# Earlier and mostly unpaced routing scatters, a first slot prepared by quarters, weights' loads ahead of its numbers

## The chip, the cores and the metric

The kernel runs on one core of a Trainium2 chip. The metric is device time in microseconds (us) from launch to end; lower is better. The engines are TensorE (PE), VectorE (DVE), ScalarE (ACT), GpSimd (POOL) and SyncE (SP); SP mostly issues DMAs. Each engine runs its own stream in the order in which the program was written, and waits on semaphores for the others.

## The reference

Three layers follow one another, all in float32.

1. Linear attention over q, k, v of shape (8, 8, 576, 64): `softmax(q)` along the head dimension, `softmax(k)` along the sequence, `kv = k_s^T v` per head, and `q_s kv`. The result is read as x with 4608 tokens of 512 numbers.
2. A mixture of 8 experts with one expert per token: `logits = x @ w_gate + bias[modality]`, the expert is the argmax, its softmax weight scales the token, and `out = gate * relu(x @ w1[e]) @ w2[e]`, w1 being 512x1024 and w2 1024x512.
3. A dense layer pair, 512 to 2048 to 512, with a leaky relu of slope 0.01; its weights arrive as float64.

## The kernel before, in words

**Attention and routing (lines 96 to 417).** Batches are taken in four pairs, each of nine chunks of 128 tokens, so 36 chunks. A chunk is transposed and exponentiated (`trans`, line 232), multiplied with its pair's `kv` (`xmm`, 239; `xp` has two buffers), divided by its sums and written to DRAM as `xd` (`evac`, 255). The last chunk of a pair takes its two halves from two batches (lines 247 to 251). Beside that, `phase_k` (137) prepares the next pair's `kv`, and `phase_q` (209) subtracts row maxima from q, in three thirds of a pair: `qmax` on DVE (218), `qsub` on POOL (222).

Routing (`phase_r`, 275) takes chunks in five groups: 0 to 8, 9 to 17, 18 to 26, 27 to 32, 33 to 35, numbered 0 to 4 here. Steps r0 to r16 compute for each token its expert, its gate and its row in a table `region` in DRAM that is ordered by expert. Nearly all of them are small DVE operations; `rm` (330) is a tiny matmul and `rx` (311) an ACT exponential. Then one indirect DMA of POOL for each chunk, the scatter (`scat`, 360), writes 128 pairs of token number and gate into `region`. A paced scatter (`paced`, 372) has a one-element POOL copy in front of it that reads the `ri` of a given chunk, so that POOL waits until attention has come that far.

The order is written by hand: every step has a time in units of chunks, the list is sorted by it (line 416), and each engine gets its instructions in that order. `route` (392) adds a group's steps at times relative to its last chunk's end, from a table, and its scatters from `ts` on, `rate` apart.

**Expert tables (`slot_tables`, 425).** From the expert counts DVE computes, in a chain of small operations that ends with the casts into `ti` (475, 476), for each slot of 512 tokens its expert, its place in `region`, and its place in the output.

**Experts (`experts`, 485).** Sixteen slots, nine of them always run. For a slot s:
- `idload` (544): SP reads 4 KB of `region` at an address that it takes from `ti`, into `idt`.
- `xload` (549): DVE casts the token numbers, and POOL issues four gathers of 128 rows of `xd` into the quarters of `xg`.
- `xgate` (557): ACT scales each quarter by the gate.
- `xprep(k)` (561): PE transposes block k of all four quarters, and `split` (480) writes it as a high part `xh` (ACT) and a rest `xl` (DVE).
- `wload` (513) loads weights in pieces of 512 KB through a ring of six buffers, on SP, at an address from `ti`. `wsplit` (534) splits a piece into high part and rest (ACT, then DVE) and lets `loads_to` (529) issue more loads. A load into a used buffer waits for the DVE half of that split.
- `pass1` (567) and `pass2` (578) multiply, each product as three matmuls of parts. `pass1` of f needs all 512 columns of `xh` and `xl`, and the w1 piece f // 2.

Between the slots' steps the float64 weights of layer 3 are converted (`conversions`, 640; loads by `f64_load`, 592). Before the first slot the program writes lines 682 to 692: the numbers of slot 0, two weight loads, the numbers of slot 1, three more loads, the gathers, the first w1 split, the gates, the four `xprep`, the other w1 splits.

**Layer 3 (`Hidden` and `last_product`).** The two dense products run after the experts, PE-bound; the change doesn't touch them.

Of the kernel before, what the change touches and what calls it, by code (L numbers as in the profile page):

```python
# [9 lines left out]
F32 = mybir.dt.float32  # L10
# [4 lines left out]
ALU = mybir.AluOpType  # L15
# [4 lines left out]
B, H, S, D = 8, 8, 576, 64  # L20
NT, DM = B * S, H * D
NE, F1, F2 = 8, 1024, 2048
NPAIR = B // 2
# [68 lines left out]
def bc(ap, axis, n):  # L92
    a = ap.unsqueeze(axis)
    shape = list(a.shape)
    shape[axis] = n
    return a.broadcast_to(shape)


def attention(ctx, tc, cst, a, region, xd):

    nc = tc.nc
    ident, onesf, trib, onesb, biasT, tokid = cst["id"], cst["one"], cst["trib"], cst["oneb"], cst["biasT"], cst["tok"]
# [9 lines left out]
    kvx = []  # L112
    for i in range(4):
        t = one.tile([128, 4, 146], F32, name=f"kvx{i}")
# [97 lines left out]
    def phase_q(i):  # L212
        s = {}

        def heads(n):
            return qt[i].rearrange("p c (h d) -> p (c h) d", d=D)[:, 24 * n:24 * n + 24]

        def qmax(n):
            qm = s[n] = sp.tile([128, 24], F32, tag="qm", name="qm")
            nc.vector.tensor_reduce(out=qm, in_=heads(n), axis=AX.X, op=ALU.max)  # L220

        def qsub(n):
            v = heads(n)
            nc.gpsimd.tensor_tensor(out=v, in0=v, in1=bc(s[n][:, :], 2, D), op=ALU.subtract)

        tm, ts = ((0.2, 3.2, 9.5), (1.2, 4.2, 10.5)) if i == 0 else ((4.6, 7.5, 11.0), (5.2, 8.5, 12.0))
        return [(t, qmax, n) for n, t in enumerate(tm)] + [(t, qsub, n) for n, t in enumerate(ts)]

    def phase_x(i):
        s = {}  # L230

        def trans(c):
            tp = ps_t.tile([128, 4, 128], F32, tag="t", name="tq")
            for hp in range(4):
                nc.tensor.transpose(out=tp[:, hp], in_=qt[i][:, c, 128 * hp:128 * hp + 128], identity=ident)
            eq = s["eq", c] = sp.tile([128, 4, 128], F32, tag="eq", name="eq", bufs=3)
            nc.scalar.activation(out=eq, in_=tp, func=AF.Exp)

        def xmm(c):
            eq = s["eq", c]  # L240
            xp = s["xp", c] = ps_x.tile([128, 4, 256], F32, tag="x", name="xp")
            if c < 8:
                kx = kvx[(2 * i + c // 4) % 4]
                for hp in range(4):
                    nc.tensor.matmul(xp[:, hp, 0:146], lhsT=eq[:, hp], rhs=kx[:, hp], start=True, stop=True)
            else:
                for j in range(2):
                    kx = kvx[(2 * i + j) % 4]
                    for hp in range(4):
                        nc.tensor.matmul(xp[64 * j:64 * j + 64, hp, 0:146], lhsT=eq[:, hp, 64 * j:64 * j + 64],  # L250
                                         rhs=kx[:, hp], start=True, stop=True)
            nc.scalar.activation(out=ri[:, NC * i + c], in_=xp[:, :, 144:146], func=AF.Identity, bias=eps[:, 0:1])
            nc.scalar.copy(out=lr[:, NC * i + c], in_=xp[:, :, 128:144])

        def evac(c):
            r = ri[:, NC * i + c]
            nc.vector.reciprocal(out=r, in_=r)
            xr = sp.tile([128, DM], F32, tag="xr", name="xr", bufs=4)
            nc.vector.tensor_tensor(out=xr.rearrange("p (q j d) -> p q j d", q=4, j=2),
                                    in0=s["xp", c][:, :, 0:128].rearrange("p q (j d) -> p q j d", j=2),  # L260
                                    in1=bc(r, 3, D), op=ALU.mult)
            if c < 8:
                r0 = (2 * i + c // 4) * S + 128 * (c % 4)
                nc.sync.dma_start(out=xd[r0:r0 + 128], in_=xr)
            else:
                for j in range(2):
                    r0 = (2 * i + j) * S + 512
                    nc.sync.dma_start(out=xd[r0:r0 + 64], in_=xr[64 * j:64 * j + 64])

        l = []  # L270
        for c in range(NC):
            l += [(c - 0.9, trans, c), (c + 0.3, xmm, c), (c + 1.0, evac, c)]
        return l
# [104 lines left out]
    def add(t0, l):  # L378
        for x in l:
            steps.append((t0 + x[0], len(steps)) + tuple(x[1:]))  # L380
# [11 lines left out]
    def route(c0, c1, times, ts, rate=0.0):  # L392


        fs, scats = phase_r(c0, c1)
        t = 0
        for n, (name, f) in enumerate(fs.items()):
            t = times.get(name, t)
            add(c1 + t, [(0.001 * n, f)])
        for n, (f, c) in enumerate(scats):  # L400
            if rate:
                at = c1 + ts + rate * n
                add(at, [(0.0, paced, min(int(at) - 1, NPAIR * NC - 1), f, c)])
            else:
                add(c1 + ts, [(0.001 * n, f, c)])

    slow = dict(r0=1.15, r1=2.5, r2=3.5, rx=4.4, r5=4.5, r8=5.6, rm=6.55, r10=6.6, r12=7.6, r13=7.61, r16=8.5)
    mid = dict(r0=0.2, r1=0.9, r2=1.2, rx=2.1, r5=2.15, r8=2.6, rm=3.3, r10=3.4, r12=4.1, r16=4.6)
    fast = dict(r0=0.2, r2=0.6, rx=1.45, r5=1.15, rm=2.25, r10=2.1, r12=2.6)
    route(0, 9, slow, 9.05, 1.0)  # L410
    route(9, 18, slow, 9.05, 0.7)
    route(18, 27, mid, 5.05, 0.5)
    route(27, 33, fast, 3.5)
    route(33, 36, dict(r0=0.2), 0.5)
    add(1.0, [(0.1, cst["prep"])])
    for x in sorted(steps, key=lambda x: x[:2]):
# [63 lines left out]
def split(nc, hi, lo, src):  # L480
    nc.scalar.copy(out=hi, in_=src)  # L481
    nc.vector.tensor_tensor(out=lo, in0=src, in1=hi.bitcast(F32), op=ALU.subtract)  # L482


def experts(ctx, tc, cst, a, region, xd, dense, did, wops, pre):
    nc = tc.nc
    ident = cst["id"]
    wp = ctx.enter_context(tc.tile_pool(name="wp", bufs=1, reuse_waits="tile"))
    ps = ctx.enter_context(tc.tile_pool(name="ps_m", bufs=3, space=PSUM, reuse_waits="tile"))
    ps2 = ctx.enter_context(tc.tile_pool(name="ps_m2", bufs=2, space=PSUM, reuse_waits="tile"))  # L490
# [6 lines left out]
    xh = wp.tile([128, 4, SLOT], F32R, name="xh")  # L497
    xl = wp.tile([128, 4, SLOT], F32R, name="xl")
# [4 lines left out]
    idts = [wp.tile([128, 4, 2], F32, name=f"idt{i}") for i in range(3)]  # L503
    idis = [wp.tile([128, 4], I32, name=f"idi{i}") for i in range(2)]
    xg = wp.tile([128, 4, DM], F32, name="xg")
# [4 lines left out]
    def reg(s, f, mx):  # L510
        return nc.values_load(ti[0:1, 3 * s + f:3 * s + f + 1], engines=[SP] + [ACT] * (f == 2), min_val=0, max_val=mx)

    def wload(s, which, c):
        t = stage[s, which, c] = ring[cnt[0] % NST]
        cnt[0] += 1
        if s not in regs:
            regs[s] = reg(s, 0, NE - 1)
        e = bass.ds(regs[s], 1)
        if which == 1:
            src = a["w1"][e, :, 256 * c:256 * c + 256].rearrange("a (k p) f -> p (a k) f", p=128)  # L520
        else:
            src = a["w2"][e, 256 * c:256 * c + 256, :].rearrange("a (k p) f -> p (a k) f", p=128)
        nc.sync.dma_start(out=t.rearrange("p (k f) -> p k f", k=4 if which == 1 else 2), in_=src)
# [5 lines left out]
    def loads_to(n):  # L529
        while nload[0] < min(n, len(items)):  # L530
            wload(*items[nload[0]])
            nload[0] += 1

    def wsplit(s, which, c):
        n = 8 * s + 4 * (which - 1) + c
        loads_to(n + 1)
        t = stage.pop((s, which, c))
        if which == 1:
            split(nc, w1h[:, :, 256 * c:256 * c + 256], w1l[:, :, 256 * c:256 * c + 256], t.rearrange("p (k f) -> p k f", k=4))
        else:  # L540
            split(nc, w2h[:, 2 * c:2 * c + 2], w2l[:, 2 * c:2 * c + 2], t.rearrange("p (k f) -> p k f", k=2))
        loads_to(n + 1 + AHEAD)

    def idload(s):
        if s < NSLOT:
            nc.sync.dma_start(out=idts[s % 3].rearrange("p t c -> p (t c)"),
                              in_=region[bass.ds(reg(s, 1, NE * NT), SLOT), :].rearrange("(p t) c -> p (t c)", t=4))
# [9 lines left out]
    def xgate(s):  # L557
        for t in range(4):
            nc.scalar.activation(out=xg[:, t], in_=xg[:, t], func=AF.Copy, scale=idts[s % 3][:, t, 1:2])

    def xprep(k):
        tp = ps2.tile([128, 4, 128], F32, tag="tp", name="tp")
        for t in range(4):
            nc.tensor.transpose(out=tp[:, t], in_=xg[:, t, 128 * k:128 * k + 128], identity=ident)
        split(nc, *(x[:, k].rearrange("d (p t) -> d t p", t=4) for x in (xh, xl)), tp)
# [90 lines left out]
    def slot(s, step=lambda: None, mid2=lambda t: None, rows=slice(0, SLOT)):  # L656
# [14 lines left out]
        for t in range(4):  # L671
# [7 lines left out]
                wsplit(s + 1, 1, t)  # L679
            step()  # L680

    idload(0)
    loads_to(2)
    idload(1)
    loads_to(AHEAD)
    xload(0)
    wsplit(0, 1, 0)
    xgate(0)
    for k in range(4):
        xprep(k)  # L690
    for c in range(1, 4):
        wsplit(0, 1, c)
    with ExitStack() as cctx:
        conv = conversions(cctx.enter_context(tc.tile_pool(name="cv", bufs=1, side="right", reuse_waits="tile")))
        next(conv)
# [418 lines left out]
```

## Time and profile before

| | us |
|---|---|
| median of three runs (1411.2 to 1411.79) | 1411.41 |
| the profiled execution | 1407.18 |
| its span | 1405.4 |
| PE busy in the span | 1306.8 (93%) |
| DVE busy | 1029.1 (73%) |
| ACT busy | 585.5 (42%) |
| POOL busy | 322.0 (23%) |

The page shows the span in 40 slices of 35 us. PE stands at 8 or 9 tenths nearly everywhere; it stands at 4 in the fifth and sixth slices (141 to 211 us), where attention ends and the experts begin, and its granted clock is 0.7 and 0.6 there. That stretch is the one that the change edits. Busy shares are averages; what a stretch is worth is read from what each engine waits for in it.

### The profile page before, as it was taken

To read this page: it belongs to the slowest core of one execution; us is meant where nothing else is said; L and a number is where in the kernel's file an instruction comes from. 1 tells how busy PE (TensorE), PEld (TensorE's weight loads), DVE (VectorE), ACT (ScalarE), POOL (GpSimd) and SP (SyncE) were. 2 spreads that over 40 slices of the span, in tenths; PEclk is the share of its full clock that TensorE was granted. 3 is DMA by queue.
4 is the path that set the end of the run, shared out by engine and by line. 5 is a ranking of instruction groups with operands and counts; after the bars stand their busy time and mean duration, and the time that the engine had idled before them with its cause. 6 is when DMAs were issued, how large, how long until landed. Compare 5 with 4: busy or idle time off the path is not lost.

```text
span 1405.4 us, 23487 instructions
## 1 busy us (share of the span) xinstructions
PE 1306.8 (93%) x9179; PEld 1219.4 (87%) x9179; DVE 1029.1 (73%) x1392; ACT 585.5 (42%) x914; POOL 322.0 (23%) x279
## 2 busy tenths in 40 slices
PE   5989449999999999998999999999989999999998
PEld 5989337778777877788999999999989999999998
DVE  4788836776777677746777777787777777877785
ACT  3656235455545554555232333323233333333332
POOL 2225820110111011100333433434311111111111
PEclk9999769999999999998999999999999999999999
DMA  9773258787977797687933333233695443444330
GB/s 374 294 284 117 69 173 283 239 256 240 299 241 261 235 297 238 217 279 234 375 136 135 126 135 130 92 150 135 262 414 179 124 133 122 149 123 134 121 120 31
DMA packets 146969, 279.56 MB, mean 199 GB/s; under 512 B 18208, under 2 KB 70432, under 8 KB 145952
## 3 DMA queue, kind: packets, MB, share of 16 engines
q1 hardware_dynamic: 122064, 208.46, 44.0%
q10 hardware_dynamic: 17232, 48.48, 8.8%
q0 software_dynamic: 7552, 21.02, 4.2%
q8 instruction: 75, 1.23, 0.4%
q14 instruction: 46, 0.38, 0.1%
HBM read 181.59 MB, written 96.32 MB: 198 GB/s over the span
## 4 chain that ended last, share of the span: by engine, by line
issue 26%; DVE 8%; PE 8%; POOL 6%; DMA 3%; ACT 1%; POOLq 0%; SPq 0%; DVEq 0%; ACTq 0%
PE hp L801 8%; POOL out L982 3%; POOL s L841 2%; DMA wi<-wid 2%; DMA hd<-ht 2%; DVE ht L814 1%; DVE ht L847 1%; DVE ht L850 1%; DVE s L838 1%; DVE x L482 1%; DVE ht L834 1%; DVE s L836 1%; POOL s L842 1%; DVE xl L482 0%; ACT ht L843 0%
## 5 line engine op out<-in xcount | busy, mean ns | idle before, releaser
L801 PE MATMUL hp<-xh,wi 128*128 128x256 f32 x1152 | 212.9, 281 | 4.4 <-DVE ht L850 2.3
L960 PE MATMUL yp<-wi,x 128*128 128x256 f32 x1152 | 191.2, 283 | 0.3 <-DVE x L482 0.3
L801 PEld LDWEIGHTS hp<-xh,wi 128*128 128x128 f32 x1152 | 179.4, 188 | 7.0 <-DVE ht L850 3.5
L960 PE MATMUL yp<-wi,wi 128*128 128x256 f32 x1200 | 178.2, 283 | 0.3 <-DVE wi L482 0.3
L801 PE MATMUL hp<-x,wi 128*128 128x256 f32 x1296 | 164.2, 286 | 8.0 <-DVEq L708 6.5
L801 PEld LDWEIGHTS hp<-x,wi 128*128 128x128 f32 x1296 | 160.7, 194 | 8.3 <-ACTq L708 6.6
L960 PEld LDWEIGHTS yp<-wi,wi 128*128 128x128 f32 x1200 | 163.5, 192 | 0.5 <-DVE wi L482 0.5
L960 PEld LDWEIGHTS yp<-wi,x 128*128 128x128 f32 x1152 | 161.5, 192 | 0.6 <-DVE x L482 0.6
L801 PE MATMUL hp<-xl,wi 128*128 128x256 f32 x576 | 160.7, 279 | 0.0
L553 POOL DMA_INDIRECT xg<-xd,idi x44 | 55.4, 1259 | 399.4 <-DVE hl L575 349.6
L572 PE MATMUL hp<-xh,w1h 128*128 128x512 f32 (+1 forms) x320 | 122.9, 384 | 12.7 <-DVE hl L575 11.6
L583 PE MATMUL yp<-hh,w2h 128*128 128x512 f32 (+1 forms) x320 | 122.9, 384 | 0.0
L572 PE MATMUL hp<-xl,w1h 128*128 128x512 f32 (+1 forms) x320 | 121.5, 380 | 0.0
L583 PE MATMUL yp<-hl,w2h 128*128 128x512 f32 (+1 forms) x320 | 121.5, 380 | 0.0
L572 PE MATMUL hp<-xh,w1l 128*128 128x512 f32 (+1 forms) x320 | 121.4, 379 | 0.0
L583 PE MATMUL yp<-hh,w2l 128*128 128x512 f32 (+1 forms) x320 | 121.4, 379 | 0.0
L982 POOL DMA_INDIRECT out<-yo,idx x36 | 47.3, 1315 | 315.4 <-DVE idx L976 294.3
L482 DVE TENSOR_TENSOR w1l<-st,w1h 128x1024 fp32r<-128x1024 f32 x44 | 53.7, 1225 | 75.2 <-ACT w1h L481 75.1
L801 PEld LDWEIGHTS hp<-xl,wi 128*128 128x128 f32 x576 | 108.0, 187 | 0.0
L814 DVE SCALAR_TENSOR_TENSOR ht<-ht 128x1024 f32<-128x1024 f32 x72 | 104.9, 1457 | 2.5
L841 POOL TENSOR_TENSOR s<-s,s 128x512 f32<-128x512 f32 x36 | 48.6, 1351 | 207.9 <-DVE s L838 155.6
L843 ACT ACTIVATE ht<-s 128x512 f32<-128x512 f32 x36 | 22.8, 633 | 149.5 <-POOL s L842 145.1
(202 smaller groups left out, 2581.4 us busy)
## 6 DMA issues: line engine op xcount, KB each, us to landing
st<-in_w SPq DMA_DIRECT2D x89, 512.0 KB, 6.0
hd<-ht ACTq DMA_DIRECT2D x72, 512.0 KB, 3.0
xt<-hd SPq DMA_DIRECT2D x18, 1024.0 KB, 5.5
hr<-hd SPq DMA_DIRECT2D x18, 1024.0 KB, 5.5
wi<-wid SPq DMA_DIRECT2D x28, 512.0 KB, 10.7
wi<-wod SPq DMA_DIRECT2D x6, 2048.0 KB, 12.7
v<-in_v SPq DMA_DIRECT2D x16, 650.0 KB, 9.9
k<-in_k SPq DMA_DIRECT2D x16, 576.0 KB, 8.8
```

Source lines behind the costliest of these rows:

```text
L482: nc.vector.tensor_tensor(out=lo, in0=src, in1=hi.bitcast(F32), op=ALU.subtract)
L553: nc.gpsimd.indirect_dma_start(out=xg[:, t], out_offset=None, in_=xd, in_offset=bass.IndirectOffsetOnAxis(ap=idi[:, t:t + 1], axis=0), bou ...
L572: nc.tensor.matmul(hp[:, rows], lhsT=w[:, k, 128 * f:128 * f + 128], rhs=x[:, k, rows], start=(n == 0), stop=(n == 11))
L583: nc.tensor.matmul(yp[:, rows], lhsT=w[:, f, 128 * d:128 * d + 128], rhs=h[:, f, rows], start=(n == 0), stop=(n == 23))
L801: self.nc.tensor.matmul(bank[:, g], lhsT=w[:, h, k, 128 * g:128 * g + 128], rhs=x[:, k], start=(n == 0), stop=(n == 5))
L814: V.scalar_tensor_tensor(out=c, in0=c, scalar=0.01, in1=c, op0=ALU.mult, op1=ALU.max)
L834: V.tensor_tensor(out=h[:, 0, 0], in0=bank, in1=s[1], op=ALU.add)
L836: V.tensor_tensor(out=s[6], in0=bank, in1=s[1], op=ALU.add)
L841: G.tensor_tensor(out=s[6], in0=s[6], in1=s[5], op=ALU.add)
L843: nc.scalar.activation(out=h[:, 1, 1], in_=s[5], func=AF.Relu)
L960: nc.tensor.matmul(bank, lhsT=x[:, k], rhs=w[i][:, h, k], start=(c == 0), stop=(c == 23))
L982: ins = nc.gpsimd.indirect_dma_start(out=out, out_offset=bass.IndirectOffsetOnAxis(ap=idi[s % 2][:, t:t + 1], axis=0), in_=y[:, t], in_off ...
```

## The change

- Routing of group 1 uses the tighter table `mid`, and its scatters begin at 5.05 chunks after the group instead of 9.05. Group 2 gets a tighter table of its own, with scatters from 3.05 on instead of 5.05. Groups 0 and 3 keep theirs, but for `rm` and the start of group 3's scatters. Of the scatters with a rate only every third is still paced.
- The last third of the last pair's `qsub` is on DVE; the `qmax` and `qsub` of pairs 1 to 3 have earlier times.
- In a pair's last chunk the two halves alternate within the loop over hp.
- Ahead of the first slot, four weight loads stand before `idload(0)`. A new function, `xfirst(t)`, takes one quarter at a time: the gate as a DVE multiplication, four transposes, one split. The four quarters alternate with the w1 splits 2 and 3; splits 0 and 1 come ahead of them.

```diff
         def qsub(n):
             v = heads(n)
-            nc.gpsimd.tensor_tensor(out=v, in0=v, in1=bc(s[n][:, :], 2, D), op=ALU.subtract)
-        tm, ts = ((0.2, 3.2, 9.5), (1.2, 4.2, 10.5)) if i == 0 else ((4.6, 7.5, 11.0), (5.2, 8.5, 12.0))
+            eng = nc.vector if (i, n) == (NPAIR - 1, 2) else nc.gpsimd
+            eng.tensor_tensor(out=v, in0=v, in1=bc(s[n][:, :], 2, D), op=ALU.subtract)
+        tm, ts = ((0.2, 3.2, 9.5), (1.2, 4.2, 10.5)) if i == 0 else ((4.6, 7.2, 10.5), (5.2, 8.0, 11.5))
...
-                for j in range(2):
-                    kx = kvx[(2 * i + j) % 4]
-                    for hp in range(4):
+                for hp in range(4):
+                    for j in range(2):
+                        kx = kvx[(2 * i + j) % 4]
                         nc.tensor.matmul(xp[64 * j:64 * j + 64, hp, 0:146], lhsT=eq[:, hp, 64 * j:64 * j + 64],
                                          rhs=kx[:, hp], start=True, stop=True)
...
-            if rate:
+            if rate and n % 3 == 0:
                 at = c1 + ts + rate * n
                 add(at, [(0.0, paced, min(int(at) - 1, NPAIR * NC - 1), f, c)])
             else:
-                add(c1 + ts, [(0.001 * n, f, c)])
+                add(c1 + ts + rate * n, [(0.001 * n, f, c)])
...
-    fast = dict(r0=0.2, r2=0.6, rx=1.45, r5=1.15, rm=2.25, r10=2.1, r12=2.6)
     route(0, 9, slow, 9.05, 1.0)
-    route(9, 18, slow, 9.05, 0.7)
-    route(18, 27, mid, 5.05, 0.5)
-    route(27, 33, fast, 3.5)
+    route(9, 18, mid, 5.05, 0.6)
+    route(18, 27, dict(r0=0.2, r1=0.6, r2=0.8, rx=1.6, r5=1.4, r8=1.7, rm=2.4, r10=2.2, r12=2.7), 3.05, 0.4)
+    route(27, 33, dict(r0=0.2, r2=0.6, rx=1.45, r5=1.15, rm=2.4, r10=2.1, r12=2.6), 2.7)
...
+    def xfirst(t):
+        nc.vector.tensor_scalar(out=xg[:, t], in0=xg[:, t], scalar1=idts[0][:, t, 1:2], scalar2=None, op0=ALU.mult)
+        tp = ps2.tile([128, 4, 128], F32, tag="tp", name="tp")
+        for k in range(4):
+            nc.tensor.transpose(out=tp[:, k], in_=xg[:, t, 128 * k:128 * k + 128], identity=ident)
+        split(nc, *(x.rearrange("d k (p t) -> d t k p", t=4)[:, t] for x in (xh, xl)), tp)
+    loads_to(4)
     idload(0)
-    loads_to(2)
     idload(1)
     loads_to(AHEAD)
     xload(0)
     wsplit(0, 1, 0)
-    xgate(0)
-    for k in range(4):
-        xprep(k)
-    for c in range(1, 4):
-        wsplit(0, 1, c)
+    wsplit(0, 1, 1)
+    for t in range(4):
+        xfirst(t)
+        if t < 2:
+            wsplit(0, 1, 2 + t)
```

## Rows read from the trace of the kernel before

**Rows 1.** Windows: stretch, PE, PEld, DVE, ACT, POOL busy (x), clock, DMA share, GB/s.
```profile
140.00:165.00 25.00, 14.15 (x92) 12.25 (x93) 21.67 (x61) 7.19 (x26) 21.06 (x34) 0.87 0.25 85
165.00:201.00 36.00, 5.23 (x20) 3.45 (x20) 12.89 (x52) 7.08 (x9) 16.28 (x18) 0.50 0.42 139
...
220.00:300.00 80.00, 78.83 (x364) 65.18 (x363) 60.17 (x73) 41.80 (x51) 5.13 (x4) 1.00 0.77 249
```

**Rows 2.** Timeline of POOL: start us, us, engine, line, operation.
```profile
148.57 2.77 POOL L224 TENSOR_TENSOR q<-q,qm 128x1536 f32<-128x1536 f32 x1
...
168.86 0.97 POOL L361 DMA_INDIRECT region<-tg,ix  x1 [0.30 <-issue]
...
179.31 0.97 POOL L361 DMA_INDIRECT region<-tg,ix  x1 [0.30 <-issue]
184.82 1.04 POOL L553 DMA_INDIRECT xg<-xd,idi  x1 [4.54 <-issue]
```

**Rows 3.** Line 546 on SP: its register operations, first and last start.
```profile
L546 SPq FUSED_REGOPS  x12: 37/37/48, 176.6 to 638.0; - x12
```

**Rows 4.** Timeline of SP's DMA issues at the start of the experts.
```profile
181.64 0.37 SPq L546 DMA_DIRECT2D idt<-region  x1
182.89 0.98 SPq L523 DMA_DIRECT2D st<-in_w  x2
184.67 0.35 SPq L546 DMA_DIRECT2D idt<-region  x1
```

**Rows 5.** DVE timeline: two full L294, an L342, the end of the tables, idi.
```profile
114.45 0.76 DVE L294 TENSOR_TENSOR lp<-lr,ri 128x576 f32<-128x576 f32 x1
...
137.27 3.40 DVE L294 TENSOR_TENSOR lp<-lr,ri 128x576 f32<-128x576 f32 x1
...
148.67 2.70 DVE L342 TENSOR_SCALAR gs<-gs 128x9 f32<-128x9 f32 x1
...
175.63 0.15 DVE L476 CAST ti<-ci 128x2 int32<-128x2 f32 x1
...
183.85 0.17 DVE L551 CAST idi<-idt 128x4 int32<-128x4 f32 x1 [8.06 <-DMA idt<-region]
```

**Rows 6.** DMA issues, KB, us to landing: idload(1), first and second weight load.
```profile
idt<-region SPq DMA_DIRECT2D x1, 4.0 KB, 3.5
...
st<-in_w SPq DMA_DIRECT2D x1, 512.0 KB, 3.5
...
st<-in_w SPq DMA_DIRECT2D x1, 512.0 KB, 4.5
```

**Rows 7.** Timeline: operations like xfirst's, and the first slot's preparation.
```profile
121.53 0.96 DVE L145 TENSOR_SCALAR k<-k,m 128x576 f32<-128x576 f32 x2
...
151.39 1.05 PE L235 MATMUL tq<-cf,q 128*128 128x128 f32 x4 [1.50 <-POOL q L224]
...
190.23 0.72 ACT L559 ACTIVATE xg<-xg,idt 128x512 f32<-128x512 f32 x1 [2.61 <-DMA xg<-xd,idi]
...
196.67 1.96 ACT L481 CAST xh<-tp 128x512 fp32r<-128x512 f32 x2 [0.57 <-PE tp L564]
197.77 2.05 DVE L482 TENSOR_TENSOR xl<-tp,xh 128x512 fp32r<-128x512 f32 x2 [8.90 <-ACT xh L481]
...
200.64 0.78 PE L572 MATMUL hp<-xh,w1h 128*128 128x512 f32 x1
...
203.17 3.49 DVE L482 TENSOR_TENSOR w1l<-st,w1h 128x1024 fp32r<-128x1024 f32 x3
```

**Rows 8.** Timeline of the stall in the first slot: SP, DVE, PE.
```profile
206.12 0.96 SPq L602 DMA_DIRECT2D w<-in_win  x2
...
215.72 0.69 DVE L618 TENSOR_SCALAR r<-w 128x1024 int32<-128x1024 int32 x1 [6.65 <-DMA w<-in_win]
...
217.79 0.50 PE L572 MATMUL hp<-xh,w1h 128*128 128x512 f32 x1 [2.31 <-DVE hl L575]
```

**Rows 9.** Timeline of PE: a pair's last chunk.
```profile
132.65 1.77 PE L250 MATMUL xp<-kvx,eq 128*64 128x146 f32 x16 [0.38 <-DVE xr L259]
```

## The prediction

> **What bounds the kernel now.** Times are us from the span's start. I read the page's 40 slices first: PE is at 8 or 9 tenths except between 141 and 211. Windows over that part come next [rows 1]. From 140 to 165 PE is busy 14.15 of 25 and DVE 21.67: the end of attention is DVE's. From 165 to 201 PE does 5.23 of 36 at a granted clock of 0.50, the lower level, 1.2 GHz. From 220 on it is busy 78.83 of 80. So what the first slot's start gains or loses is carried to the end at full price, and the stretch up to the first expert matmul, at 200.64 [rows 7], is read on its waits.
>
> The timelines then give a chain. DVE finishes `ti` at 175.78 [rows 5]. SP has its address at 176.6 [rows 3] and could issue some 0.2 later; call that E = 176.8. But `idload(0)` leaves at 181.64 [rows 4], because POOL's last scatter starts only at 179.31 [rows 2]: POOL runs without a gap from the `qsub` at 148.57 on. The numbers land 2.2 later (DVE's `idi`, 183.85 [rows 5]), the first gather starts at 184.82 [rows 2], and its rows are there when ACT's first gate starts, 190.23 [rows 7]. From there to the first matmul it is 10.4.
>
> **The scatters.** POOL's backlog goes. Nine scatters stand between the starts at 168.86 and 179.31 [rows 2], 1.31 apart. Groups 1 and 2 begin four and two chunks sooner and lose their copies; so group 3, whose rows I put at about 163, finds POOL free, and the last of its six and group 4's three starts near 163 + 8 x 1.31 = 173.5. Landing takes 181.64 - 179.31 = 2.3 at most, so all is there by 176, before E: the wait of 181.64 - 176.8 = 4.8 goes. Late next are the weights' loads, since they now stand in front.
>
> **The end of attention.** POOL's `qsub` holds DVE up. L294 takes 0.76 in one group and 3.40 in the next, where it starts beside a `qsub`; L342, nine numbers a row, takes 2.70 beside the one at 148.57 [rows 5, 2]. Moving that last `qsub` to DVE takes away 2.5 (2.70 less about 0.2). It costs 1536 elements at the rate of `w1l` (3.49 / 3 for 1024 [rows 7]): 1.75; the bounds are 1.3 at L145's rate (0.48 for 576 [rows 7]) and POOL's own 2.8. The PE wait of 1.50 for it [rows 7] goes too, but DVE sets this end, so I count nothing. The L294 block of 2.6 I expect back at another operation: five of group 1's scatters now stand in front of the `qsub` before it, which so starts near 140 and meets group 2's two-input operations. I take -0.2 (ends -2.6 and 0). Group 1's last twelve small operations, at least 0.15 each like `ti`'s cast [rows 5], 1.8 in all, move from chunks 23 to 26 into 20 to 22, where the page has PE at 9 tenths (105 to 140) and PE may wait for DVE more; what DVE gains later it may lose there: 0 (ends -1.8 and +1.8). Sum: -2.5 + 1.75 - 0.2 = -0.9, ends -4 and +2.
>
> **The swapped loops of the last chunk.** Sixteen PE passes of 1.77 in all [rows 9], one such row a pair, and three of the four stand where PE is the bound. Order alone changes no pass: 0. As an upper end I keep +0.6, an estimate, a third of one such row for going from half to half at each pass; the lower end is the rival below.
>
> **Weights in front.** Four loads and a register load stand ahead of `idload(0)`. Two loads take SP 0.98, and from their end at 183.87 to the next `idload`, register included, it is 0.80 [rows 4]: `idload(0)` leaves at E + 4 x 0.55 + 0.8 = E + 3.0. If it landed in 2.2, it would be there at E + 5.2. But `idload(1)`, issued at 184.67 behind two loads, took 3.5 [rows 6]: it landed at 188.17, just after the second load (183.49 + 4.5 = 188.0), 5.1 after the first load's issue. The first took 3.5, so a load takes 1.6 more; the fourth lands at E + 3.5 + 3 x 1.6 = E + 8.3, and the 4 KB with it. I take E + 8.3. Before it was at 183.85, E + 7.05. So the 4.8 that POOL gives is spent: +1.3 net. The end on the other side is -1.9.
>
> The Trainium skill ("DMA: Bandwidth & Descriptors", section on queues, rings and completion order) says that each DMA engine takes the descriptors of a ring in order, though completions need not follow it. By the first half the numbers come behind the weights, +1.3; by the second alone they could come at issue + 2.2, -1.9. The row of `idload(1)` bears out the first.
>
> The gathers then meet two to four weight loads instead of six. The first took 5.4 from its start to the gate; with less beside it I estimate 4.6 (ends 3.5 and 7): -0.8.
>
> **Quarter by quarter.** `xfirst` puts DVE at both ends of each quarter: multiplication, PE's transposes, ACT's copy, DVE's subtraction. DVE runs in program order, so the multiplication of quarter t + 1 stands behind the subtraction of quarter t, and that waits for PE and ACT. Per quarter: 0.43 for the multiplication (0.48 x 512 / 576); 1.05 for four transposes at the low clock (L235 at 151.39); 0.98 for the copy and 1.03 for the subtraction (halves of 1.96 and 2.05 [rows 7]); 0.26 for three hand-overs, ACT to DVE being 197.77 - 197.65 = 0.12. That is 3.75. Four make 15.0, and two w1 splits between them add 2 x 1.16 on DVE: 17.3 from the first quarter's arrival until `xl` is whole. The gathers' later arrivals, 1.3 apart at issue, hide in that. `pass1` needs all four quarters of `xl` in its second matmul, so its start counts as 16.9 after the arrival, where before it was 10.4: +6.5. Before, the gates were ACT's and ran as gathers landed, and the `xprep`s overlapped on three engines. The ends: 15.5 if each hand-over is free, 18.5.
>
> PE is colder in it, too: fewer transposes shortly before `pass1`. At 200.64 the first matmuls take 0.78 and less, later 0.39 to 0.50 [rows 7, 8]; I add 0.5 (ends 0 and 1.2).
>
> **The first slot's stall.** The first float64 load leaves at 206.12, behind a weight load that waits for w1 split 2; DVE stands 6.65 for it, until 215.72, and PE 2.31 until 217.79 [rows 8]. In the new order split 2 is done near E + 19, some 10 ahead of `pass1`: the stall goes, -2.4 (end 0).
>
> **The sum** on the profiled execution (1407.18, span 1405.4): -0.9 + 1.3 - 0.8 + 6.5 + 0.5 - 2.4 = +4.2. That execution is 4.2 below the runs' median, 1411.41; added to the median the forecast is 1415.6.
>
> **Rivals.**
> - *The quarters overlap after all* (the other side). If quarter t + 1's multiplication doesn't wait for quarter t's subtraction, the preparation ends one chain after the last gather: about 4.0 + 3.75 after the first arrival, 7.4 in place of 16.9. Sum 4.2 - 9.5 = -5.3: 1406.1. It decides once the preparation takes less than 17.3 - 4.2 = 13.1. For it: the gathers land one by one, and the first gate waited for its own alone [rows 7]. Against: DVE's `w1l` of the splits 1 to 3 starts only at 203.17, in written order [rows 7]. 10%.
> - *The numbers pass the weights.* Landing at E + 5.2, less about 1.0 of gather time lost to the weights: 4.2 - 3.1 + 1.0 = +2.1: 1413.5. Against it is `idload(1)`. 10%.
> - *The lock doesn't come back.* The `qsub` that meets group 2 falls beside reductions and PSUM operations alone; DVE gains 2.4 more: +1.8, 1413.2. For it: reductions and operations on PSUM are most of DVE's time there. 14%.
> - *The halves run side by side.* If passes on the two column halves overlapped, each last chunk would give 0.9, three of them -2.7: 4.2 - 2.7 = +1.5, 1412.9. For it: the halves write different partitions; against: the before row's passes are already 0.11 apart, less than any full-width pass. 6%. The Trainium skill ("TensorEngine Tiling (Array Packing)", key properties) says that tiles work independently and can load weights and multiply in parallel; no run so far shows it.
> - *POOL comes too late for PE.* Group 1's first scatter waits for its rows and stands, with eight more, in front of two `qsub`s that PE's transposes need. If each comes 2 to 3 late where PE is the bound: +3, 1418.6. 16%.
>
> **How the numbers follow.** The forecast has 44% and runs from 1413.8 to 1417.6. About 0.2%, 2.8, is what a measurement tells from no change, so the line to "same" is at 1414.2. Faster: the overlap, 10%, and 3% from others at their ends: 0.13. Same: lock, halves and numbers, 30%, less those 3%, with a little of the forecast's low end, 2%: 0.29. Slower: 0.58. The range from 1408.5 to 1420 leaves out the overlap and the far end of POOL's rival. The likeliest case alone is 1413.8 to 1417.6.
>
> **What would show it.** SP's `idt` without a wait for `region`, but landing with the fourth weight load, about 8 after the first load's issue. DVE alternating multiplication, idle, subtraction over some 17 before the first L572; that matmul at about 205 to 206. No DVE wait for `in_win` in the first slot. No 2.70 at L342. Wrong it is if the preparation takes under 13, or if the numbers land by E + 6.

## The result, and the profile after

The changed kernel takes 1423.82 us (median of four runs, 1420.51 to 1426.46) against 1411.6 for the kernel before: a ratio of 1.0080, 95% interval 1.0062 to 1.0097. It is slower, by 12.2 where 4.2 was forecast. Its profiled execution took 1420.51, span 1418.7, 13.3 more than the profiled one of before, where the sum said +4.2.

The same windows as [rows 1], of after, and one more between them:

```profile
140.00:165.00 25.00, 16.51 (x106) 15.30 (x106) 18.30 (x42) 7.70 (x29) 17.33 (x20) 0.84 0.24 74
165.00:201.00 36.00, 3.84 (x25) 2.71 (x25) 16.59 (x71) 4.31 (x11) 14.46 (x14) 0.50 0.51 161
201.00:220.00 19.00, 7.62 (x21) 5.25 (x22) 7.82 (x10) 5.50 (x6) 2.16 (x3) 0.50 0.57 193
220.00:300.00 80.00, 78.84 (x356) 65.02 (x355) 57.44 (x71) 41.20 (x52) 6.94 (x6) 0.99 0.68 214
```

From 220 on nothing has changed. The hole in PE's work has grown: it now lasts to about 215, and the granted clock is still at 0.50 in the whole of 201 to 220. The start of the experts in after, on SP and DVE, to set beside [rows 4, 5, 7]:

```profile
182.48 0.16 DVE L476 CAST ti<-ci 128x2 int32<-128x2 f32 x1
184.33 1.79 SPq L523 DMA_DIRECT2D st<-in_w  x4
187.00 1.49 SPq L546 DMA_DIRECT2D idt<-region  x2
193.00 0.17 DVE L551 CAST idi<-idt 128x4 int32<-128x4 f32 x1 [10.37 <-DMA idt<-region]
...
198.69 0.67 DVE L684 TENSOR_SCALAR xg<-xg,idt 128x512 f32<-128x512 f32 x1 [3.25 <-DMA xg<-xd,idi]
201.66 1.09 DVE L482 TENSOR_TENSOR xl<-tp,xh 128x512 fp32r<-128x512 f32 x1 [2.29 <-ACT xh L481]
...
203.77 0.51 DVE L684 TENSOR_SCALAR xg<-xg,idt 128x512 f32<-128x512 f32 x1
206.58 1.09 DVE L482 TENSOR_TENSOR xl<-tp,xh 128x512 fp32r<-128x512 f32 x1 [2.30 <-ACT xh L481]
...
215.35 1.06 DVE L482 TENSOR_TENSOR xl<-tp,xh 128x512 fp32r<-128x512 f32 x1 [2.36 <-ACT xh L481]
```

SP no longer waits for the scatters: its first DMA leaves 1.7 after `ti`. But that is a weight load, and the numbers are in use 8.67 after it. Then the quarters go one after another: a multiplication, about 2.3 of waiting for ACT, a subtraction, and only then the next multiplication, 17.7 from the first to the end of the last.

The table gives starts in the traces: DVE's evacuation (L259, L260 in after) of chunks 19, 27 and 35, the end of `ti`, `idi`, and the first L572 of the first and second slot. Differences along a row are what to read; the spans begin up to 2 apart, before any edit acts.

| | chunk 19 | 27 | 35 | ti | idi | L572 | second slot |
|---|---|---|---|---|---|---|---|
| before | 117.18 | 142.20 | 163.78 | 175.78 | 183.85 | 200.64 | 249.72 |
| after | 115.04 | 145.96 | 170.92 | 182.64 | 193.00 | 215.37 | 264.09 |
| e3 | 117.90 | 142.94 | 170.55 | 182.13 | 193.21 | 217.16 | 266.06 |
| e4 | 117.59 | 148.23 | 175.74 | 188.01 | 190.87 | 208.10 | 259.23 |
| e5 | 118.04 | 143.75 | 174.19 | 185.98 | 189.46 | 206.69 | 256.41 |
| e6 | 118.88 | 150.29 | 173.85 | 185.59 | 193.84 | 211.39 | 260.62 |
| e7 | 116.70 | 141.74 | 169.13 | 180.72 | 191.70 | 209.70 | 258.29 |
| e8 | 117.66 | 148.13 | 173.93 | 186.19 | 196.84 | 210.95 | 262.13 |
| e9 | 116.57 | 141.59 | 162.09 | 173.62 | 183.07 | 200.04 | 251.13 |
| e10 | 116.47 | 141.50 | 162.01 | 173.52 | 182.86 | 199.59 | 246.02 |
| e13 | 118.50 | 152.75 | 177.23 | 188.79 | 196.64 | 213.25 | 262.47 |
| e16 (before again) | 117.35 | 142.39 | 168.78 | 180.38 | 188.42 | 206.02 | 255.58 |
| e17 | 117.11 | 142.08 | 161.61 | 173.03 | 179.17 | 196.45 | 243.22 |

Before to after at the second slot's start is +14.4: -2.1 up to chunk 19 (the traces are that far apart at chunk 7 already), +5.9 from chunk 19 to 27, +3.4 from 27 to 35, -0.3 to `ti`, +7.9 from `ti` to L572, -0.4 in the first slot. Later 1.1 comes back.

### The profile page after: what moved, and what is told of

Read it like the earlier page. It is cut to its first block, busy times and chain, and to the rows that moved or that the text cites. A ratio compares the mean times of both kernels' runs of the same rounds, so it can differ in the third digit from the quotient of the medians.

```text
span 1418.7 us, 23454 instructions
## 1 busy us (share of the span) xinstructions
PE 1307.4 (92%) x9179; PEld 1221.3 (86%) x9179; DVE 1031.4 (73%) x1397; ACT 582.3 (41%) x910; POOL 315.1 (22%) x260
## 4 chain that ended last, share of the span: by engine, by line
issue 27%; DVE 9%; POOL 6%; PE 5%; DMA 4%; ACT 1%; POOLq 0%; SPq 0%; DVEq 0%; ACTq 0%
PE hp L809 5%; POOL out L990 3%; POOL s L849 2%; DMA wi<-wid 2%; DMA hd<-ht 2%; DVE ht L822 2%; DVE ht L855 1%; DVE ht L858 1%; DVE s L846 1%; DVE ht L842 1%; DVE s L844 1%; DVE x L482 1%; POOL s L850 1%; DVE xl L482 0%; DVE xt L795 0%
## 5 line engine op out<-in xcount | busy, mean ns | idle before, releaser
L572 PE MATMUL hp<-xh,w1h 128*128 128x512 f32 (+1 forms) x320 | 123.3, 385 | 11.1 <-DVE hl L575 9.3
L572 PE MATMUL hp<-xl,w1h 128*128 128x512 f32 (+1 forms) x320 | 122.3, 382 | 0.3 <-DVE xl L482 0.3
L572 PE MATMUL hp<-xh,w1l 128*128 128x512 f32 (+1 forms) x320 | 122.1, 382 | 0.0
```

What stands on the lines that cost most here:

```text
L572: nc.tensor.matmul(hp[:, rows], lhsT=w[:, k, 128 * f:128 * f + 128], rhs=x[:, k, rows], start=(n == 0), stop=(n == 11))
```

## Experiments

Differences in the text are of medians, each against the kernel before on the same chip; the intervals are in this table.

| run | median us | before | ratio (95%) |
|---|---|---|---|
| e1 | 1426.64 | 1413.11 | 1.0092 (1.0077 to 1.0107) |
| e2 | 1413.47 | 1413.11 | 1.0004 (0.9994 to 1.0014) |
| e3 | 1423.32 | 1413.11 | 1.0066 (1.0053 to 1.0079) |
| e4 | 1415.90 | 1413.11 | 1.0013 (1.0002 to 1.0023) |
| e5 | 1414.13 | 1413.13 | 1.0007 (0.9998 to 1.0016) |
| e6 | 1418.51 | 1413.13 | 1.0049 (1.0036 to 1.0062) |
| e7 | 1416.20 | 1413.13 | 1.0019 (1.0009 to 1.0030) |
| e8 | 1417.94 | 1413.13 | 1.0037 (1.0024 to 1.0050) |
| e9 | 1407.32 | 1410.07 | 0.9988 (0.9977 to 0.9998) |
| e10 | 1403.81 | 1410.07 | 0.9958 (0.9945 to 0.9972) |
| e11 | 1416.47 | 1410.07 | 1.0048 (1.0032 to 1.0064) |
| e12 | 1407.15 | 1410.07 | 0.9981 (0.9971 to 0.9991) |
| e13 | 1418.48 | 1413.51 | 1.0034 (1.0021 to 1.0047) |
| e14 | 1410.91 | 1413.51 | 0.9988 (0.9976 to 1.0000) |
| e15 | 1412.64 | 1413.51 | 0.9990 (0.9981 to 0.9999) |
| e17 | 1401.14 | 1409.16 | 0.9937 (0.9923 to 0.9950) |
| e18 | 1404.45 | 1409.16 | 0.9961 (0.9947 to 0.9974) |

### The change taken apart: e1 to e4

e1 is after with the old loops, e2 is before with the swapped ones:

```diff
-                for hp in range(4):
-                    for j in range(2):
-                        kx = kvx[(2 * i + j) % 4]
+                for j in range(2):
+                    kx = kvx[(2 * i + j) % 4]
+                    for hp in range(4):
```

> The changed kernel with the last chunk's loops back in the old order (j outside). Theory A (alternating the two column halves upsets TensorE late in attention: after's trace has waits put down to 'remote' at L189, L253 and L238 that before has not, and its runs spread over 6 us): the waits go, `ti` is done 5 to 7 sooner, the time falls to about 1417 and the runs agree within 1.5. Theory B (the tighter routing of groups 1 and 2 makes the loss, by TensorE's waits for it and for POOL): the four last chunks' passes are slower again (4 x 0.55 = 2.2 at most), nothing else changes: 1423 to 1426, with the spread kept.

> The kernel before with the swapped loops of the last chunk alone. Theory A: slower than before by 3 to 7, 1415 to 1418, with waits put down to 'remote' in the trace. Theory B: L251's sixteen passes take 1.22 in place of 1.77, up to 4 times 0.55: 1409.5 to 1411.5, runs within 1.

Theory A fell. e1 is no faster than after (+13.5), and e2 is level with before (+0.4); waits put down to "remote" appear without the swap too (e16 below). The swap does one thing, seen in the sixteen passes of one pair's last chunk, before and then e2:

```profile
102.29 1.77 PE L250 MATMUL xp<-kvx,eq 128*64 128x146 f32 x16
```

```profile
101.23 1.22 PE L250 MATMUL xp<-kvx,eq 128*64 128x146 f32 x16
```

That is 0.55 a pair. In e2's time nothing of it is left.

e3 is before with the diff's last hunk alone (`xfirst`, weights in front); e4 is before with the hunks of `phase_q` and `route` alone.

> The kernel before with the first slot's part alone (weights in front, quarter by quarter). Both theories, from the prediction's terms: numbers still behind POOL's last scatter (181.6) or behind four weights (176.8 + 8.3 = 185.1), so +1.2; gathers -0.8; chain +6.5; colder start +0.5 to +1.3; stall -2.4: +5 to +6, 1416.5 to 1417.5. If after's loss has a share in the first slot that those terms miss, it is over 1419.

> The kernel before with the earlier routing, the earlier mostly unpaced scatters and the q subtractions of the change alone: loops and first slot as before. Theory A: the scatters no longer hold up the numbers (-4.8) and attention ends 0.9 sooner: -5.7, about 1406. Theory B: attention ends 6 to 8 later, of which the scatters' 4.8 come back: +1 to +3, 1413 to 1415.

e3 is +10.2: the first slot is the larger part, and dearer than its terms (+5 to +6). In its trace the numbers are in use 11.08 behind `ti`, in before 8.07: the weights leave first, and `idload(0)` still waits for the scatters until 191.42. The gathers take 7.45 from there to the first multiplication, and the slot itself gains 0.2 where the terms had 1.1 to 1.9. e4 is +2.8, theory B. Its trace has what the change was to give, the numbers right behind `ti`:

```profile
187.85 0.16 DVE L476 CAST ti<-ci 128x2 int32<-128x2 f32 x1
189.30 0.36 SPq L546 DMA_DIRECT2D idt<-region  x1
190.87 0.17 DVE L551 CAST idi<-idt 128x4 int32<-128x4 f32 x1 [2.86 <-DMA idt<-region]
```

2.9 from `ti` to `idi` in place of 8.1. But chunk 27 comes 30.6 behind chunk 19, and 25.0 in every trace with the old routing.

### Group 1's routing: e5, e6, e11, e13

```diff
 e5: e4 with the swapped loops, all scatters of group 1 paced, and
-    route(9, 18, mid, 5.05, 0.6)
+    route(9, 18, slow, 9.05, 0.7)
 e6: before, group 1 paced at every third scatter, and
-    route(9, 18, slow, 9.05, 0.7)
+    route(9, 18, mid, 5.05, 0.6)
```

> The changed kernel's attention, but with group 1's routing and its paced scatters at their old times, and with the first slot's part as before (so: swapped loops, groups 2 and 3, the q subtractions). Theory G1 (moving group 1 into chunks 20 to 22 makes the loss of the attention part: TensorE waits 2.8 for its rows and then runs at 0.5 of the clock; e4's evacuation of chunk 27 is 6.1 later than e3's, against 0.8 sooner at chunk 17): 5 to 6 come back from e4's 1415.9, and the swap gives 1: 1409 to 1411. Rival Q (the q subtractions and groups 2 and 3 make it): 1414 to 1416.

> The kernel before with group 1's earlier, mostly unpaced routing alone. Theory G1: attention ends 5 to 6 later, POOL's shorter backlog gives back 0 to 3: 1415.5 to 1419. Rival Q: 1411.5 to 1413.5, as before or better.

e6 is +5.4: by itself, group 1's move costs that. Chunk 27 is 31.4 behind chunk 19; in e5 it is 25.7. But e5's time (+1.0) misses theory G1 and lies where rival Q put it: with group 1 back only 1.8 of e4's +2.8 is gone. It loses in chunks 27 to 35, 30.4 apart against 20.5 to 27.6 in the traces with before's attention (of that spread, e16 below). Three traces from one chip, each one execution with e16's stall, bear on it: chunk 35 stands 52.43 behind chunk 19 in e7 (old routing), 56.15 in e5 (groups 2 and 3 moved) and 56.27 in e8 (group 1 moved too). So there group 1's old place gives nothing back by the end of attention, and the losses don't add up. Whether groups 2 and 3 make the loss in e5 or the stall does (ACT stands 5.65, 2.53 and 4.99 for it in e5, 8.08 in e7) is not shown: what groups 2 and 3 cost by themselves was not run. The timeline of e6, all engines, shows how group 1 hurts:

```profile
120.00 3.46 DVE L321 TENSOR_TENSOR oh<-w,mx 128x72 f32<-128x72 f32 x1
120.59 2.77 POOL L224 TENSOR_TENSOR q<-q,qm 128x1536 f32<-128x1536 f32 x1
123.56 0.17 DVE L173 RECIPROCAL rk<-rk 128x2 f32<-128x2 f32 x1
123.76 1.28 ACT L180 ACTIVATE kvx<-kvp,rk 64x64 f32<-64x64 f32 x4 [4.21 <-DVE rk L173]
125.09 0.17 PE L332 MATMUL rp<-tb,trib 128*128 128x8 bf16 x1 [4.21 <-ACT kvx L180]
125.15 4.08 PE L166 MATMUL kvp<-v,ek 128*128 128x130 f32 x20
```

Read it from the first row down. L321, 72 numbers a row, takes 3.46 beside the `qsub`; elsewhere it takes 0.28. The reciprocal behind it in DVE's order (`krec`, L173) is late, so ACT's `kvx` is late, and that frees the PSUM bank that PE's rank matmuls need: PE stands 4.21. In after the same three steps cost L316 2.01, beside the `qsub` at 114.82, and PE 2.82:

```profile
114.82 2.75 POOL L225 TENSOR_TENSOR q<-q,qm 128x1536 f32<-128x1536 f32 x1 [3.50 <-DVE qm L220]
115.65 2.01 DVE L316 SCALAR_TENSOR_TENSOR w<-lg,cf 128x72 f32<-128x72 f32 x1
119.87 0.17 PE L333 MATMUL rp<-tb,trib 128*128 128x8 bf16 x1 [2.82 <-ACT kvx L180]
119.92 4.68 PE L166 MATMUL kvp<-v,ek 128*128 128x130 f32 x20
```

After the pause PE works at the lower level: windows of the same stretch, after and then before.

```profile
119.00:126.00 7.00, 6.13 (x31) 6.13 (x31) 6.30 (x17) 1.61 (x6) 2.25 (x3) 0.51 0.21 75
```

```profile
119.00:126.00 7.00, 6.70 (x59) 6.49 (x58) 6.41 (x17) 4.10 (x14) 4.94 (x5) 1.00 0.28 98
```

31 recorded passes in the time of 59. The Trainium skill ("SBUF — State Buffer", section on the two separate sides) says that VectorE, in an operation with two SBUF inputs, and a GpSimd operation that reads SBUF hold a port pair exclusively, for the whole instruction. L321 agrees: it ends 0.1 behind the `qsub`.

e11 and e13, each e6 with one more line changed, ask whether a better place saves it:

```diff
-    route(9, 18, mid, 5.05, 0.6)
+    route(9, 18, dict(mid, rm=4.3, r12=5.1, r13=5.11, r16=5.6), 6.05, 0.6)                             # e11
+    route(9, 18, dict(mid, r5=3.1, r8=3.5, rm=4.3, r10=4.35, r12=5.1, r13=5.11, r16=5.6), 6.05, 0.6)   # e13
```

> e6 (group 1 moved, +5.4) with the rank matmuls and all behind them, the scatters too, one chunk later. Theory P (the loss is TensorE's own wait for the rank matmuls' input, 4.2 at 125.1 in e6, and the slow clock after it): 4 to 5 come back, 1413.5 to 1415. Theory D (the loss is VectorE's: a dozen small operations more in chunks 19 to 22, where it is the next bound, whatever TensorE waits at): 0 to 1 comes back, 1417.5 to 1419.

> e11 with group 1's one-hot operations (r5 to r9) a chunk later too, so that they are issued behind the q subtraction of chunk 21 and not beside it. Theory L (the loss is POOL's: e11's L321 took 3.45 in place of 0.28 beside the q subtraction that starts at 118.94, and what stands behind it on VectorE, the reciprocals that free TensorE's bank, comes that much later): L321 takes 0.3, chunk 20 is evacuated about 3 sooner, 2.5 to 3.5 come back from e11's +6.4, so +3 to +4 against before. Theory D (a dozen small operations more where VectorE is full, wherever they stand): +5.5 to +6.5.

e11 gives nothing back (+6.4). e13 does at its place what theory L said: L321 takes 0.28 and chunk 20 comes 1.25 behind chunk 19, in e11 5.57. But now PE waits at another place, and after that the next `qsub` meets the next operation with two inputs (e13, DVE, POOL and PE):

```profile
124.15 0.28 DVE L321 TENSOR_TENSOR oh<-w,mx 128x72 f32<-128x72 f32 x1
126.48 1.75 DVE L220 TENSOR_REDUCE qm<-q 128x24 f32<-128x1536 f32 x1
129.15 0.16 DVE L345 TENSOR_TENSOR oh<-rp,cf 128x8 f32<-128x8 f32 x1
129.36 0.47 PE L161 MATMUL kvp<-cf,k 128*128 128x128 f32 x1 [3.70 <-DVE oh L345]
129.70 3.40 DVE L352 TENSOR_TENSOR st<-st,oh 128x72 f32<-128x72 f32 x1
130.23 2.77 POOL L224 TENSOR_TENSOR q<-q,qm 128x1536 f32<-128x1536 f32 x1
```

PE's 3.70 is again the PSUM bank, held for `rp` until L345 reads it, and L345 stands late in DVE's order, behind a `qmax` of 1.75 and an evacuation. It has nothing to do with the lock: the `qsub` starts at 130.23, when PE's wait is over. e13 is +5.0, between the theories. So the place of one operation is not the cause: moved by itself into chunks where PE is the bound and DVE nearly full, group 1's chain costs 5 to 6 at all three places that I tried.

### The first slot: e7, e8

```diff
 e7: e3 with xfirst split into xmul and xtr, and
+    xmul(0)
     for t in range(4):
-        xfirst(t)
+        if t < 3:
+            xmul(t + 1)
+        xtr(t)
 e8: e4 with
-    idload(0)
-    loads_to(2)
+    loads_to(4)
+    idload(0)
```

> e3 (first slot's part alone) with the multiplication of quarter t+1 written ahead of the subtraction of quarter t. Theory O (VectorE's written order makes the quarters a chain: a multiplication stands behind a subtraction that waits 2.3 for ScalarE's copy; four rounds take 17.7): the rounds overlap, 17.7 becomes about 11 (0.7 + 1.1 + 1.1 + 1.1 + 3 x 1.6 and two w1 splits at 1.2): -5 to -7 from e3's 1423.3, 1416.5 to 1418.5. Rival (the chain is held by the copies, the slow clock or the gathers): 0 to -1.5, 1422 to 1423.3.

> e4 (routing part alone) with four weight loads in front of the numbers' load, the preparation as before. Theory W (the numbers land with the fourth load: 10.4 after `ti` in after, 2.9 in e4): +6.5 to +7.5 from e4's 1415.9, 1422 to 1423.5. Rival (the weights' own landing bounds the first matmul anyway, or the gathers gain what the numbers lose): 0 to +2.5, 1416 to 1418.5.

e7 is +3.1 where e3 is +10.2: the written order on DVE is worth 7. The wait of 2.3 ahead of the subtractions is gone, and the quarters follow 2.5 apart (e7, DVE):

```profile
202.15 1.11 DVE L482 TENSOR_TENSOR xl<-tp,xh 128x512 fp32r<-128x512 f32 x1
...
204.69 1.11 DVE L482 TENSOR_TENSOR xl<-tp,xh 128x512 fp32r<-128x512 f32 x1
...
207.21 1.10 DVE L482 TENSOR_TENSOR xl<-tp,xh 128x512 fp32r<-128x512 f32 x1
...
209.68 1.06 DVE L482 TENSOR_TENSOR xl<-tp,xh 128x512 fp32r<-128x512 f32 x1 [1.37 <-ACT xh L481]
```

11.4 from the first multiplication (199.35) to the end of the last subtraction, forecast 11; after has 17.7.

e8 is +4.8, 2.0 more than e4 by the medians, 3.4 by the ratios: less than theory W, and by the medians in the rival's range. `idi` does come 10.65 behind `ti`, in e4 2.86. But from `idi` to L572 it is 14.1 in place of 17.2, with the weights issued first.

### What pays: e9, e10, e12, and the parts together

e9 is before with `if rate and c0 < 18`, so that group 2 is not paced. e10 adds:

```diff
     wsplit(0, 1, 0)
-    xgate(0)
-    ...
     with ExitStack() as cctx:
         conv = conversions(...)
         next(conv)
+        xgate(0)
+        ...
```

> The kernel before with one edit: group 2's nine scatters lose their copies and with them the wait for a late chunk's numbers; every time of the routing stays. Theory S (the scatters' wait is worth its 4.8 by itself, and was lost only because the routing was moved for it): `ti` as before, the numbers 3 to 3.5 after `ti` in place of 7.6 to 8.1: -4 to -5, 1408 to 1409.5. Rival (unpaced scatters hold POOL for the q subtractions or VectorE, or the weights set the first matmul): 0 to -1.5, 1411.5 to 1413.

> e9 with the first float64 load issued ahead of the gates (so ahead of the weight load that waits for w1 split 1). Theory: the stall in the first slot goes (VectorE 6.6 to 7.1, TensorE 2.1 to 3.1 for it): -2 to -3 from e9. Rival (the 1 MB load takes the gathers' bandwidth, which the first slot pays at its start): -0.5 to +1.

e9 is -2.8 (-1.7 by the ratio), half of theory S or less, and not by its mechanism: the numbers still leave at 180.77, because POOL's scatters, group 1's still paced, run without a gap from 150 to 179.3, and `idi` stands 9.45 behind `ti`, in before 8.07. Where the gain comes from is not shown. e10 is -6.3, and e18, the same kernel on another chip, -4.7 (-5.5 by the ratio), where -6 was forecast for a trace like its own, without e16's stall. The float64 load leaves at 186.32, DVE's wait for it is gone, and the second slot starts 46.4 behind the first, in e9 51.1.

e12 is before with the hunk of `phase_q` alone.

> The kernel before with the change's q subtractions alone (the last on VectorE, the others half a chunk sooner). The prediction's term: -2.5 + 1.75 - 0.2 = -0.9, 1412 to 1412.5. Rival (VectorE sets the end of attention, so its 1.75 counts, and the lock it was to avoid comes back elsewhere): +1 to +2.5, 1414 to 1415.5.

-2.9: more than the term's -0.9, and the rival (slower) fell. The trace doesn't show where it is gained: `ti`, `idi` and POOL's last scatter (179.31) stand as in before.

```diff
 e14: e10 and e12, and
-            if rate and c0 < 18:
+            if rate and c0 < 9:
-    route(9, 18, slow, 9.05, 0.7)
+    route(9, 18, slow, 9.05, 0.4)
 e15: e14 with the swapped loops
 e17: e14 with
-    route(27, 33, fast, 3.5)
+    route(27, 33, fast, 3.4)
```

> A version from the single results: the kernel before with e12's q subtractions, e10's early float64 load, and groups 1 and 2 scattered without copies at their old routing times. e9 left POOL busy without a gap from 139 to 178 (27 scatters of 1.28, 13 copies, a q subtraction); here 27 scatters alone, so the last starts at about 174 and no longer holds the numbers: e10's -6.2, -1 for the q part and -3 to -4: -10 to -11. If the scatters only start later for it, or the weights bound the first matmul: -6 to -8.

> e14 with the last chunk's swapped loops. e2's chunks 9 and 18 were evacuated 0.55 and 1.1 sooner, and lost it by the end; with the end of attention on the path, -1 from e14. If VectorE or the slow TensorE of chunks 33 to 35 takes it again: 0.

> e14 with group 3's scatters a tenth of a chunk sooner. In e14, as before, groups 3 and 4 are due at the same time (36.5) and so alternate in POOL's order: POOL stood 7.4 at 170 for group 4's rows with five of group 3's scatters behind, and the numbers' load left at 189.3, 5.9 after `ti`. With group 3 ahead, five scatters of 1.28 fall into that gap, the last starts 1.3 x 3 after group 4's rows, and the load leaves about 1.7 after `ti`, as in after: -4 from e14, -5.5 to -7 against before. Rival (the weights then set the first matmul): -0 to -1 from e14.

e14 (-2.6) and e15 (-0.9) missed. In e14's POOL the reason stands in one wait:

```profile
169.02 0.97 POOL L362 DMA_INDIRECT region<-tg,ix  x1 [1.24 <-DVE ix L359]
177.40 0.98 POOL L362 DMA_INDIRECT region<-tg,ix  x1 [7.41 <-issue]
```

33 + 3.5 and 36 + 0.5 are the same time, so groups 3 and 4 alternate, and five scatters whose rows are ready stand behind one whose row is not; `ix` of group 4 is done at 176.6. The numbers then leave 5.9 behind `ti`; in e4, where nothing holds them, it is 1.3, so the tie costs at most 4.6 there, an estimate. The order is the same in before, where POOL's backlog hides it. With group 3 a tenth of a chunk ahead, e17 is the best: 1401.14, -8.0, against -4.7 for e18 on the same chip. That this is the tie's doing is not shown. e17's trace lacks the stall that e14's has (chunk 35 at 161.61, there at 171.81, on another chip), its scatters run from 140 on without a gap over 0.32, and the numbers leave 4.5 behind `ti`, where 1.7 was forecast: there the scatters, 1.28 apart, set the time (e17's `ti`, last scatter and load):

```profile
172.87 0.16 DVE L477 CAST ti<-ci 128x2 int32<-128x2 f32 x1
175.25 0.97 POOL L362 DMA_INDIRECT region<-tg,ix  x1 [0.30 <-issue]
177.58 0.36 SPq L547 DMA_DIRECT2D idt<-region  x1
```

> e10 again, on e17's chip, to compare the two: against before -4 to -6 where TensorE stalls late in attention as in e16's trace, -6 where it doesn't.

### Before once more: e16

> The kernel before, profiled once more. e3 and e7 have the same attention, and there chunk 35 is evacuated 14.7 to 14.9 behind chunk 32, in before's first profile 8.25, and e9 7.8. If that is one chip's or one execution's doing, this trace shows either value with nothing changed; `ti` between 173.5 and 182.

This is the unchanged kernel, one execution of 1415.02 on the chip of e13 to e15; the chip of the first profile is not on record. Up to chunk 33 each evacuation is 0.1 to 0.2 behind the first trace; then chunk 34 comes 7.4 behind chunk 33, where it was 2.4. ACT's `ri` of that chunk, in e16 and in before:

```profile
165.48 0.27 ACT L252 ACTIVATE ri<-xp,eps 128x8 f32<-128x8 f32 x1 [5.81 <-remote]
```

```profile
157.82 0.27 ACT L252 ACTIVATE ri<-xp,eps 128x8 f32<-128x8 f32 x1 [0.34 <-PE xp L245]
```

PE's matmuls for it are recorded at 156.80 to 157.96 in e16:

```profile
156.80 1.16 PE L245 MATMUL xp<-kvx,eq 128*128 128x146 f32 x8
```

Chunk 35 is 19.5 to 21.6 behind chunk 27 in six traces with the routing's old step times (before, e9, e10, e12, e17, e18) and 26.4 to 29.8 in six more (e2, e3, e7, e14 to e16). So the first profile was spared a stall of about 5 that half of these executions have, which fits its 4.2 below its own runs' median, and the stall is there without the change. The second six come from three chips on which before's median is 1413.1 to 1413.5, five of the first six from two on which it is 1409.2 and 1410.1: it may go with the chip, which is not shown (e6, on one of the three, has no wait put down to "remote" there, nor has e11 on one of the two). In after the same sign stands a chunk earlier, in ACT's `ri` of chunk 33 and `eq` of chunk 35:

```profile
163.40 0.27 ACT L253 ACTIVATE ri<-xp,eps 128x8 f32<-128x8 f32 x1 [4.29 <-remote]
166.31 0.60 ACT L238 ACTIVATE eq<-tq 128x512 f32<-128x512 f32 x1 [2.54 <-remote]
```

A step of 1.2 to 4.1 at chunk 33 stands in all five traces with groups 2 and 3 moved (after, e1, e4, e5, e8) and in e15 alone of the others; whether the new times bring the stall forward is open.

## Why the prediction was wrong

The direction was right, and the place; the size was off by 9 in the profiled sum.

- **The step that failed** is the end of attention, -0.9 with ends -4 and +2; it measured +6.9 at `ti`: -2.1 by which the traces are apart before any edit acts, +5.9 from chunk 19 to 27, -1.0 to chunk 32, +4.4 to chunk 35, -0.3 to `ti`. In it, "Group 1's last twelve small operations" were put at 0 with ends at 1.8 to either side, and e6, with that move alone, is +5.4. I priced their own busy time. What they cost is PE's time between chunks 19 and 27, by a chain that the text had in pieces: the lock, which I expected back at another operation but sized as DVE's alone; DVE's written order, in which `krec` stands behind it; the PSUM bank; the low clock after the pause. For the earlier steps of group 2 the sum had no cost but the lock's, and e5 loses without group 1's move too. How the +6.9 divides between group 1, groups 2 and 3, and the stall stays open, as e5 and e6 don't add up. The +4.4 behind chunk 32 has the sign of e16's stall, which no term had and before's profile did not show.
- The `qsub` on DVE, -2.5 + 1.75 - 0.2 in the same step, was too low: e12, which also has the earlier times of `qmax` and `qsub`, gives -2.9.
- The scatters' wait went, as forecast, and e4's `idi` 2.9 behind `ti` bears it out. But POOL's last scatter starts at 182.19 in after, not at 173.5: group 3's rows came at 170.6, not at 163, and only `ti` being as late hid it.
- Weights in front, +1.3: the landing at E + 8.3 was right (8.67 behind the first load's issue), but that load left 1.7 after `ti`, not 1.0: +2.3. The gathers' -0.8 measured -0.7.
- Quarter by quarter, +6.5, was right: 16.7 from the first multiplication to L572 for 16.9, and 17.7 for 17.3 to the last `xl`. e7 shows the cause, DVE's order.
- The colder PE, +0.5 with ends 0 and 1.2, was too small. L572 reaches its steady 0.4 after twelve passes and 5.96 in after, after five and 2.19 in before; at 0.227 a pass that is 3.2 lost for 1.05: +2.2, of which 0.7 is the wait for the last `xl`. The stall's -2.4 came (no DVE wait for `in_win`), and the two leave -0.4 in the slot for my -1.9.
- The rivals: "the halves run side by side" was right in its mechanism, 1.22 for 1.77, and worth 0 in e2 and 1 to 2 between e1 and after, whose intervals overlap. "The lock doesn't come back" fell: it came back at L316 and, as expected, at group 2's L310, beside the `qsub` that starts near 140. "POOL comes too late for PE" named the right victim, PE in the chunks around 20, with the wrong cause.

```profile
141.20 3.23 DVE L310 TENSOR_TENSOR lg<-lg,mx 128x72 f32<-128x72 f32 x1
141.56 2.77 POOL L225 TENSOR_TENSOR q<-q,qm 128x1536 f32<-128x1536 f32 x1
```

## What to carry to other kernels

An operation moved into a stretch is priced by what stands behind it on its engine and who waits for that, down to the PSUM bank, not by its own length. Before work is moved earlier to free a queue, read the order inside the queue: in e14 five ready scatters stood behind one that was not, by a tie in the due times. One profile is one execution; where it lies apart from its own runs' median, profile the unchanged kernel again before its margins are used.

## What the hardware showed unexpectedly

- Late in attention PE's results reach ACT long after the recorded end of the matmuls (7.5 in e16, 157.96 to 165.48), while DVE is busy for 0.20 and ACT for 0.51 of the 5 us from 161. The granted clock is 0.99 from 155 to 161 and 0.59 from 161 to 166, so the lower level alone doesn't explain a matmul group of 1.16 that ends so late. The profile models the ends of matmuls, so the recorded end may be off. It is there in one execution of a kernel and not in another. What it is stays open; e3 and e16 have it with neither the swap nor the new routing.
- Alternating two halves of the columns runs sixteen passes in 1.22 for 1.77. The Trainium skill ("TensorEngine Tiling (Array Packing)", key properties) says that tiles work in parallel; these rows agree, but don't show which part overlaps.
- A `qsub` stretches whichever operation of DVE with two inputs in SBUF it meets, however small: 0.28 to 3.46 (L321), and an operation on nine numbers to 2.70 [rows 5]. Reductions and operations with one input in PSUM beside it kept their length (1.34 for L142, 0.69 for the evacuations).
